# Attention rows of two batches, laid singly along the steps of the second expert

## The chip, the cores and the metric

The kernel runs on one core of a Trainium2 chip. The time is the device time of one execution in microseconds (us); the profile is of one execution of its own. A core has TensorE (PE; its weight loads are shown apart as PEld), VectorE (DVE), ScalarE (ACT), GpSimd (POOL) and SyncE (SP), whose queue issues most DMAs here. Each engine runs its own instructions in order; semaphores order the engines among each other.

## The reference

There are three stages. The first is attention with 4 batches, 8 heads, 576 rows and a head size of 64, in which a score under its row's maximum less `tau` is dropped. The attention's output, 2304 tokens of 512 values, goes through two experts of 2048 hidden values one after the other; the second one's output is the result.

```python
scores = scale * np.matmul(q, k.transpose(0, 1, 3, 2))
thresh = np.max(scores, axis=-1, keepdims=True) - tau
scores = np.where(scores >= thresh, scores, -1e9)      # then a softmax, and attn @ v
...
h = x @ w_in                                           # first expert
g = (a0 + a1*h + a2*h**2 + a3*h**3) / (1 + |b0|*|h| + |b1|*h**2 + 1e-6)
x = g @ w_out
...
h = x @ w_in                                           # second expert
g = np.where(h >= 1, h, np.where(h <= -1, 0, (h + 1)**2 / 4))
return g @ w_out
```

## The kernel before

The experts set the beat. The work is cut into 192 steps: for each of the four batches a phase of the first expert and then one of the second (`m` 0 and 1), in each phase three blocks of 192 tokens (`j`) and eight chunks of 256 hidden values (`i`), so 24 steps a phase. In the code batches count from 0, in the text from 1: batch 3 is `b` 2. Steps 48 to 71 are the first expert of batch 2, 72 to 95 its second expert, 96 to 119 and 120 to 143 the two of batch 3.

A step has a first product (L889, 24 matmuls of 192 columns), the activation, a split of the result into two half-precision parts (L210 on ScalarE, L214 on GpSimd), and three steps later (`LAG`) the second product (L905, 24 matmuls). The activation is `rational` in the first expert, with six VectorE operations (L750, L751, L752, L755, L760, L761) and ScalarE's, first of them L748; in the second expert it is `quadratic`, with one on ScalarE (L812) and two on VectorE (L813, L814). The weights lie in eight buffers; while a phase's last eight steps run, the chunks of the next expert are loaded into them, 1 MB each, from the SP queue.

Attention of the first batch stands before the steps. That of batches 2 to 4 is laid beside the steps of the batches before: the generator `attention(b)` gives work in units, and `spread` hands these out evenly over the steps in `ATTENTION`, as first step, step of the first row, and end. A batch has preparation (`prep_pair` loads two heads' q and k, scales and splits them and transposes them by DMA; `prep_v` does the same for v without a transpose) and then, for each of four pairs of heads, nine rows of scores (`ROWS`), three a unit. A row is a chain over all engines:

- scores (L397, L398, TensorE, into a PSUM tile of which there is one),
- the maximum (L445, VectorE), the two constants (L446 ScalarE, L447 VectorE),
- the exponential (L404, ScalarE) and the threshold (L405, VectorE),
- the split (L413 ScalarE, L414 and twice L416 GpSimd) into `hl`,
- a transposing DMA from the SP queue into `eT` (L418; three buffers),
- the weighted sums with v (L431, sets of 14 matmuls; the ninth row has two sets),
- after each second row and the ninth, `normalize` (L466 to L480), which transposes the result on TensorE (L471) and writes it to `xT`, the input of the first expert.

The order on each engine is made at build time by a scheduler that simulates the program and, among what is ready, issues what has the earliest priority. `at(t)` sets a priority by step. A first product has its step's, a second product 1.5 steps more, a unit of attention 1.5 steps less than its place, and the weighted sums of batches 3 and 4 three steps more than their unit. Priority is no barrier: what is ready early may be issued early. `tc.issue_after(x)` is one: what is traced under it on the engine of `x` is issued behind `x`. Before the change only the second products stand under it.

Of the kernel before, what the change touches and what calls it, by code (L numbers as in the profile page):

```python
# [10 lines left out]
F32 = mybir.dt.float32  # L11
I32 = mybir.dt.int32
BF16 = mybir.dt.bfloat16
AF = mybir.ActivationFunctionType
ALU = mybir.AluOpType
# [6 lines left out]
LARGEST = 3e38  # L22
# [12 lines left out]
N_TEMP, N_POLY, N_WT, N_WH, N_GG, N_ROW, N_SC = 5, 3, 3, 2, 4, 3, 2  # L35


PREPARE = 1, 6
ATTENTION = {1: (18, 18 + 32 * 3 / 17, 50), 2: (51, 67, 100), 3: (99, 115, 147)}
PREPARED = 3  # L40
WEIGHTS = (0, 20)


@with_exitstack
def tile_attention_moe_moe2(
# [18 lines left out]
    V, A, G, T, Q = nc.vector, nc.scalar, nc.gpsimd, nc.tensor, nc.sync  # L64
    B, H, S, D = q.shape
    P = 128
    NP = H // 2
    NT = S // P
    ST = S - NT * P
# [16 lines left out]
    ap = ctx.enter_context(tc.tile_pool(name="ap", bufs=2))  # L86
# [4 lines left out]
    ps_1 = ctx.enter_context(tc.tile_pool(name="ps_1", bufs=1, space=PSUM))  # L91
    ps_2 = ctx.enter_context(tc.tile_pool(name="ps_2", bufs=1, space=PSUM))
# [17 lines left out]
    def small(n, name, keep=False):  # L110
        if keep:
            return cp.tile([P, n], F32, name=name)
        tag = "".join(x for x in name if x.isalpha() or x == "_").rstrip("_")
        return sp.tile([P, n], F32, name=name, tag=f"s{n}_{tag}", bufs=4 if tag in ("mx", "nt") else 2)
# [38 lines left out]
    ln_e = small(1, "ln_e", True)  # L153
# [23 lines left out]
    def at(when):  # L177

        return tc.high_priority(tc.cur_priority - int(1000 * (when + 100)))
# [200 lines left out]
    ROWS = [(t, ab) for t in range(NT) for ab in range(2)] + [(NT, 0)]  # L380
    M = NT * P

    def scores(s, t, ab, qT, kT, kT2):

        if t < NT:
            parts = [(slice(0, P), ab * (NT + 1) + t, slice(0, P), [(ab * S, S)])]
        else:
            parts = [(slice(i * ST, (i + 1) * ST), NT, slice(i * ST, (i + 1) * ST),
                      [(0, S)] if i == 0 else [(S + ST, M), (S, ST)]) for i in range(2)]
        k1 = kT.rearrange("p c s -> p (c s)")  # L390
        k2 = kT2.rearrange("p c s -> p (c s)")
        for rows, c, cols, keys in parts:
            at = 0
            for k0, n in keys:
                while n:
                    w = min(n, 512 - at % 512)
                    T.matmul(s[rows, at : at + w], qT[:, c, cols], k1[:, k0 : k0 + w], start=True, stop=False)  # L397
                    T.matmul(s[rows, at : at + w], qT[:, c, cols], k2[:, k0 : k0 + w], start=False, stop=True)  # L398
                    at, k0, n = at + w, k0 + w, n - w

    def softmax(b, s, ab, con, nb, th, name):

        e = ap.tile([P, S], F32, name="e" + name, tag="e", bufs=N_SC)
        A.activation(e, s, AF.Exp, bias=nb, scale=con[:, 0:1])  # L404
        V.scalar_tensor_tensor(e, s, th, e, op0=ALU.is_ge, op1=ALU.mult)  # L405
        hl = ap.tile([P, 2 * S], F16, name="hl" + name, tag="hl", bufs=N_ROW)
        if ab == 0:

            hi, whole, half, lo_w, lo_h = hl[:, 0:S], slice(0, M), slice(M, S), hl[:, S + ST :], hl[:, S : S + ST]
        else:  # L410

            hi, whole, half, lo_w, lo_h = hl[:, S:], slice(ST, S), slice(0, ST), hl[:, 0:M], hl[:, M:S]
        A.copy(hi, e)  # L413
        G.tensor_tensor(lo_h, e[:, half], hi[:, half], op=ALU.subtract)  # L414
        for p in (slice(0, M // 2), slice(M // 2, M)):
            G.tensor_tensor(lo_w[:, p], e[:, whole][:, p], hi[:, whole][:, p], op=ALU.subtract)  # L416
        eT = ap.tile([P, C, P], F16, name="eT" + name, tag="eT", bufs=N_ROW)
        Q.dma_start_transpose(out=eT, in_=hl)  # L418
        return eT

    def weighted(pv, rows, eT, cols, vv, h, ab):

        his, los = [(c, c) for c in range(NT)], [(NT + 1 + c, c) for c in range(NT)]
        if ab:
            his, los = los, his
        blocks = []
        for c, x in [(NT, NT)] + his:
            blocks += [(c, x, 0, D + 1), (c, x, D + 1, D)]
        blocks += [(c, x, 0, D + 1) for c, x in los]
        for n, (c, x, at, w) in enumerate(blocks):  # L430
            T.matmul(pv[rows, 0:w], eT[:, c, cols], vv[:, h * NT + x if x < NT else H * NT + h, at : at + w], start=(n == 0), stop=(n == len(blocks) - 1))  # L431

    now = [0]

    def att_rows(b, pr, g, data, pvs):

        con, qT, kT, kT2, vv, h = data
        name = f"{b}_{pr}_{g}"
        rows = ROWS[3 * g : 3 * g + 3]
        for r, (t, ab) in enumerate(rows):  # L440
            banks = ps_2.tile([P, 1024], F32, name=f"s{name}_{r}", tag="s")
            scores(banks, t, ab, qT, kT, kT2)
            mx, nt = small(1, f"mx{name}_{r}"), small(2, f"nt{name}_{r}")
            s = ap.tile([P, S], F32, name=f"sc{name}_{r}", tag="sc", bufs=N_SC)
            V.tensor_scalar(s, banks[:, 0:S], 1.0, -LARGEST, op0=ALU.mult, op1=ALU.max, accum_out=mx)  # L445
            A.activation(nt[:, 1:2], mx, AF.Identity, bias=ln_e, scale=con[:, 1:2])  # L446
            V.tensor_scalar(nt[:, 0:1], mx, con[:, 2:3], None, op0=ALU.add)  # L447
            eT = softmax(b, s, ab, con, nt[:, 1:2], nt[:, 0:1], f"{name}_{r}")
            if ab == 0:
                pv = ps_1.tile([P, 512], F32, name=f"pv{b}_{pr}_{t}", tag="pv")  # L450
                pvs[t] = pv[:, 0 : 2 * (2 * D + 2)].rearrange("p (a d) -> p a d", a=2)
            with at(now[0] + 3) if b > 1 else nullcontext():
                if t < NT:
                    weighted(pvs[t][:, ab], slice(0, P), eT, slice(0, P), vv, h + ab, ab)
                else:
                    for i in range(2):
                        c = slice(i * ST, (i + 1) * ST)
                        weighted(pvs[t][:, 0], c, eT, c, vv, h + i, 0)
                if ab == 1 or t == NT:
                    normalize(b, pr, t, pvs.pop(t))  # L460

    def normalize(b, pr, t, pv):
        name = f"{b}_{pr}_{t}"
# [16 lines left out]
            V.tensor_tensor(dst[:, 1], pt[r, c : c + w], dst[:, 0], op=ALU.subtract)  # L480

    NG = len(ROWS) // 3
    N_UNITS = NP * (NG + 1) + 1

    def attention(b):

        ahead = [prep_pair(b, 0)]
        yield
        vv = prep_v(b)
        yield  # L490
        xT[b] = [xp.tile([P, 2 * KT, TB], F16, name=f"xT{b}_{j}", tag="xT", bufs=NB) for j in range(NB)]
        ahead.append(prep_pair(b, 1))
        yield
        for pr in range(NP):
            pvs = {}
            data = ahead.pop(0) + (vv, 2 * pr)
            for g in range(NG):
                att_rows(b, pr, g, data, pvs)
                yield
                if g == 1 and pr + 2 < NP:  # L500
                    ahead.append(prep_pair(b, pr + 2))
                    yield


    def first_v():
# [422 lines left out]
    def spread(first, last, units):  # L928
        for n, u in enumerate(units):
            t = first + n * (last - first) / len(units)  # L930
            beside[int(t)].append((t, u))

    for b, (first, rows, last) in ATTENTION.items():
        spread(first, rows, [("att", b)] * PREPARED)
        spread(rows, last, [("att", b)] * (N_UNITS - PREPARED))
    spread(*WEIGHTS, [("w", i, x) for i in range(NCH) for x in range(2)])

    pending, consts, accs, atts = [], {}, {}, {}
# [15 lines left out]
    for st, (n, m, b, j, i) in enumerate(steps):  # L954
        with at(st):
            if i == 0:
                if m == 0:
                    consts[m, b, j] = moe1_consts(b) if j == 0 else consts[m, b, 0]
                else:
                    if b == 0 and j == 0:  # L960
                        moe2_weights()
                    consts[m, b, j] = moe2_consts(b, j)
            gg, last = first_product(m, b, j, i, consts[m, b, j])
        pending.append((n, m, b, j, i, gg, last))
        if len(pending) > LAG:
            with at(st + 1.5):
                finish_step()
        for t, u in beside[st]:
            if u[0] == "w":
                with at(t - 3):  # L970
                    stage_half(1, u[1], u[2], False)
            else:
                if u[1] not in atts:
                    atts[u[1]] = attention(u[1])
                now[0] = t - 1.5
                with at(now[0]):
                    next(atts[u[1]])
    while pending:
        with at(st + 1.5):
# [29 lines left out]
```

## Time and profile before

| | |
|---|---|
| median of 3 executions | 1236.87 us (1236.17 to 1237.26) |
| the profiled execution | 1231.83 us, span 1230.0 us |
| PE, PEld busy | 1094.3 us (89%), 989.2 us (80%) |
| DVE busy | 977.6 us (79%) |
| ACT, POOL busy | 839.2 us (68%), 553.4 us (45%) |
| granted TensorE clock, mean | 0.965 |

The shares are means over the whole span. Which engine is full changes from phase to phase, so the rows below are cut at the phases.

### The profile page before, as it was taken

The numbers are of one execution on the slowest core, as the hardware profiler recorded it, in microseconds if no ns is written. First come the engines' busy times: TensorE is split into PE (matmuls) and PEld (weight loads), VectorE is DVE, ScalarE is ACT, GpSimd is POOL, SyncE is SP. The second block draws the span as 40 slices with busy tenths as digits, with TensorE's granted clock in tenths as the row PEclk, the third lists the DMA queues.
The fourth block names the chain that finished last, engine by engine and source line by source line (L and its number), as shares of the span: only waits on it lengthen the run. The fifth ranks groups of instructions, "written<-read, shape, count | busy, mean of one in ns | idle before, by whom it ended". The sixth has DMA issues, their size and how long they took to land.

```text
span 1230.0 us, 31762 instructions
## 1 busy us (share of the span) xinstructions
PE 1094.3 (89%) x12636; PEld 989.2 (80%) x12636; DVE 977.6 (79%) x2365; ACT 839.2 (68%) x1532; POOL 553.4 (45%) x698
## 2 busy tenths in 40 slices
PE   2878788588899999998899998988999998999998
PEld 1445555477889988997889898987888998999998
DVE  8887996999997387799995767899987777896432
ACT  2677777798886377788764776888666676775332
POOL 2445455666665166224553564234564652222221
PEclk9889888799999999999999999999999999999999
DMA  7677667644278159734492559333775476007000
GB/s 228 220 224 243 228 243 254 208 116 115 50 191 210 34 117 198 206 101 93 112 277 42 111 93 240 115 78 70 233 177 92 79 193 187 10 2 269 8 14 27
DMA packets 217845, 175.51 MB, mean 143 GB/s; under 512 B 179680, under 2 KB 190944, under 8 KB 209504
## 3 DMA queue, kind: packets, MB, share of 16 engines
q1 hardware_dynamic: 216320, 171.12, 52.5%
q8 instruction: 99, 1.62, 0.5%
q10 hardware_dynamic: 1376, 2.36, 0.5%
q14 instruction: 50, 0.41, 0.1%
HBM read 106.83 MB, written 21.50 MB: 104 GB/s over the span
## 4 chain that ended last, share of the span: by engine, by line
PE 39%; DVE 31%; ACT 10%; DMA 7%; issue 7%; POOL 5%; SPq 1%; ACTq 0%; DVEq 0%; POOLq 0%
PE acc L905 15%; PE ph L889 15%; DMA eT<-hl 3%; DVE e L405 3%; DVE t L755 3%; DVE t L750 2%; DVE sc L445 2%; PE pv L431 2%; DVE t L761 2%; POOL wh L214 2%; PE pv L617 2%; DVE t L760 2%; DVE t L751 2%; DVE t L752 2%; DVE wt L232 1%
## 5 line engine op out<-in xcount | busy, mean ns | idle before, releaser
L905 PE MATMUL acc<-gg,wc 128*128 128x192 f16 x4608 | 426.1, 247 | 12.8 <-POOL gg L214 6.1
L889 PEld LDWEIGHTS <-wc 128*128 128x128 f16 x4608 | 391.2, 99 | 30.0 <-issue 24.3
L905 PEld LDWEIGHTS <-wc 128*128 128x128 f16 x4608 | 385.0, 98 | 13.7 <-issue 12.0
L214 POOL TENSOR_TENSOR gg<-t,gg 128x384 f16<-128x384 f32 x192 | 195.9, 1023 | 382.2 <-ACT gg L210 307.9
L889 PE MATMUL ph<-xT,wc 128*128 128x192 f16 x2304 | 217.8, 252 | 14.4 <-DVE t L752 14.0
L889 PE MATMUL ph<-yT,wc 128*128 128x192 f16 x2304 | 214.4, 247 | 7.1 <-DVE t L814 4.1
L416 POOL TENSOR_TENSOR hl<-e,hl 128x256 f16<-128x256 f32 x216 | 162.5, 772 | 0.0
L210 ACT CAST gg<-t 128x384 f16<-128x384 f32 x192 | 97.1, 508 | 85.2 <-DVE t L814 44.8
L813 DVE SCALAR_TENSOR_TENSOR t<-t,c 128x384 f32<-128x384 f32 x96 | 64.6, 673 | 93.9 <-ACT t L812 92.2
L405 DVE SCALAR_TENSOR_TENSOR e<-sc,nt,e 128x576 f32<-128x576 f32 x108 | 95.1, 881 | 23.3 <-ACT e L404 22.6
L414 POOL TENSOR_TENSOR hl<-e,hl 128x64 f16<-128x64 f32 x108 | 47.4, 439 | 130.3 <-ACT hl L413 121.5
L404 ACT ACTIVATE e<-sc,nt,con 128x576 f32<-128x576 f32 x108 | 93.4, 865 | 4.8 <-POOL hl L416 0.2
L445 DVE TENSOR_SCALAR_CACHE_REDUCE sc<-s 128x576 f32<-128x576 f32 x108 | 80.8, 748 | 16.8 <-PE s L398 16.3
L812 ACT ACTIVATE t<-ph,c 128x384 f32<-128x384 f32 x96 | 64.0, 667 | 41.3 <-PE ph L889 40.9
L413 ACT CAST hl<-e 128x576 f16<-128x576 f32 x108 | 72.1, 668 | 27.4 <-DVE e L405 27.0
L431 PE MATMUL pv<-v,eT 128*128 128x65 f16 (+3 forms) x1680 | 75.1, 194 | 17.4 <-DMA eT<-hl 15.9
L431 PEld LDWEIGHTS <-eT 128*128 128x128 f16 (+1 forms) x1680 | 65.5, 100 | 24.1 <-DMA eT<-hl 18.7
L214 POOL TENSOR_TENSOR wc<-wt,wc 128x256 f16<-128x256 f32 x64 | 54.9, 890 | 61.0 <-ACT wc L210 61.0
L748 ACT ACTIVATE t<-ph,sc 128x384 f32<-128x384 f32 x96 | 55.2, 575 | 38.8 <-PE ph L889 38.2
L753 ACT ACTIVATE t<-t,lc 128x384 f32<-128x384 f32 x96 | 67.7, 708 | 19.6 <-DVE t L750 18.8
L214 POOL TENSOR_TENSOR wh<-wt,wh 128x256 f16<-128x256 f32 x64 | 59.0, 952 | 35.3 <-ACT wh L210 35.2
L750 DVE SCALAR_TENSOR_TENSOR t<-t,qc 128x384 f32<-128x384 f32 x96 | 69.1, 720 | 6.9 <-ACT t L748 6.8
(244 smaller groups left out, 1907.6 us busy)
## 6 DMA issues: line engine op xcount, KB each, us to landing
wc<-scratch SPq DMA_DIRECT2D x56, 1024.0 KB, 6.2
rw<-in_moe_w_in_dram SPq DMA_DIRECT2D x15, 1024.0 KB, 5.6
rw<-in_moe_w_out_dram SPq DMA_DIRECT2D x15, 1024.0 KB, 5.4
scratch<-wc SPq DMA_DIRECT2D x8, 1024.0 KB, 4.5
scratch<-wh SPq DMA_DIRECT2D x16, 512.0 KB, 3.6
rqk<-in_q_dram SPq DMA_DIRECT2D x16, 256.0 KB, 2.9
rqk<-in_k_dram SPq DMA_DIRECT2D x16, 256.0 KB, 3.1
kT<-qkT SPq DMA_DIRECT2D x26, 144.0 KB, 2.6
```

What stands on the lines that cost most here:

```text
L210: A.copy(hi, src)
L214: G.tensor_tensor(lo[:, p], src[:, p], hi[:, p], op=ALU.subtract)
L404: A.activation(e, s, AF.Exp, bias=nb, scale=con[:, 0:1])
L405: V.scalar_tensor_tensor(e, s, th, e, op0=ALU.is_ge, op1=ALU.mult)
L413: A.copy(hi, e)
L416: G.tensor_tensor(lo_w[:, p], e[:, whole][:, p], hi[:, whole][:, p], op=ALU.subtract)
L431: T.matmul(pv[rows, 0:w], eT[:, c, cols], vv[:, h * NT + x if x < NT else H * NT + h, at : at + w], start=(n == 0), stop=(n == len(blocks) ...
L445: V.tensor_scalar(s, banks[:, 0:S], 1.0, -LARGEST, op0=ALU.mult, op1=ALU.max, accum_out=mx)
L750: V.scalar_tensor_tensor(u, u, qc[:, 0:1], u, op0=ALU.add, op1=ALU.mult)
L753: A.activation(r, u, AF.Ln, bias=lc[:, 1:2], scale=lc[:, 0:1])
L889: last = T.matmul(ph[:, f, :], w[:, wx, kt, f * P : (f + 1) * P], rhs, start=(n == 0), stop=(n == 3 * KT - 1))
L905: T.matmul(dst, w[:, wx, f, d * P : (d + 1) * P], gg[:, gx, f, :], start=(i == 0 and f == 0 and n == 0 and d % 2 == 0), stop=(i == NCH - 1 ...
```

## The change

For batches 3 and 4 a unit is now one row in place of three, and the units of rows lie on steps 72.3 to 97 and 120.3 to 145 (before: 67 to 100 and 115 to 147). The preparation lies on the steps ahead of that. A row's weighted sums are held back and traced behind the scores of the row three later (`BEHIND`); their own priority of three steps more is gone. The last three rows' sums are a unit of their own. All units from the first row on stand under `tc.issue_after(last)`, where `last` is the last matmul of the step's first product. Batch 2 keeps three rows a unit with the sums at once.

```diff
-ATTENTION = {1: (18, 18 + 32 * 3 / 17, 50), 2: (51, 67, 100), 3: (99, 115, 147)}
+ATTENTION = {1: (18, 18 + 32 * 3 / 17, 50), 2: (51, 72.3, 97), 3: (99, 120.3, 145)}
+BEHIND = 3
...
+    def sums_of(b, pr, t, ab, h, vv, eT, pvs):
+        if ab == 0:
+            pv = ps_1.tile([P, 512], F32, name=f"pv{b}_{pr}_{t}", tag="pv")
+            pvs[t] = pv[:, 0 : 2 * (2 * D + 2)].rearrange("p (a d) -> p a d", a=2)
+        if t < NT:
+            weighted(pvs[t][:, ab], slice(0, P), eT, slice(0, P), vv, h + ab, ab)
+        else:
+            for i in range(2):
+                c = slice(i * ST, (i + 1) * ST)
+                weighted(pvs[t][:, 0], c, eT, c, vv, h + i, 0)
+        if ab == 1 or t == NT:
+            normalize(b, pr, t, pvs.pop(t))
+
+    def att_row(b, pr, r, data, pvs):
...
+        eT = softmax(b, s, ab, con, nt[:, 1:2], nt[:, 0:1], name)
+        return partial(sums_of, b, pr, t, ab, h, vv, eT, pvs)
...
-            with at(now[0] + 3) if b > 1 else nullcontext():
...
-    N_UNITS = NP * (NG + 1) + 1
+    N_UNITS = {b: NP * ((NG if b == 1 else len(ROWS)) + 1) + (1 if b == 1 else 2) for b in range(1, B)}
...
+        held = []
         for pr in range(NP):
             pvs = {}
             data = ahead.pop(0) + (vv, 2 * pr)
-            for g in range(NG):
-                att_rows(b, pr, g, data, pvs)
-                yield
-                if g == 1 and pr + 2 < NP:
+            for r in range(len(ROWS)):
+                held.append(att_row(b, pr, r, data, pvs))
+                if b == 1 or len(held) > BEHIND:
+                    held.pop(0)()
+                if b > 1 or r % 3 == 2:
+                    yield
+                if r == 5 and pr + 2 < NP:
                     ahead.append(prep_pair(b, pr + 2))
                     yield
+        for f in held:
+            f()
+        yield
...
-                now[0] = t - 1.5
-                with at(now[0]):
+                with at(t - 1.5), tc.issue_after(last) if u[1] > 1 and t >= ATTENTION[u[1]][1] else nullcontext():
                     next(atts[u[1]])
```

A batch has 42 units, 3 of preparation ahead of the rows and 39 from the first row on: 36 rows, the preparation of pairs 3 and 4, and the last sums. 39 units on 24.7 steps are 0.633 steps each.

## Rows read from the trace of the kernel before

**Rows 1.** Busy us of each engine by stretch: start:end, length, engines, granted clock, DMA share, GB/s.
```profile
495.70:551.00 55.30, 52.71 (x650) 51.07 (x648) 48.74 (x116) 45.62 (x86) 12.92 (x17) 1.00 0.57 149
551.00:624.60 73.60, 64.50 (x785) 59.95 (x784) 73.60 (x181) 57.05 (x111) 37.60 (x46) 0.98 0.51 127
624.60:762.60 138.00, 128.35 (x1690) 119.62 (x1688) 95.89 (x264) 86.10 (x166) 66.21 (x96) 0.99 0.66 144
684.70:762.60 77.90, 72.83 (x997) 66.82 (x994) 52.71 (x139) 52.87 (x101) 41.22 (x65) 1.00 0.74 162
762.60:812.30 49.70, 49.52 (x620) 48.68 (x618) 44.92 (x107) 41.71 (x80) 12.88 (x16) 1.00 0.39 114
812.30:884.30 72.00, 61.56 (x733) 57.37 (x732) 71.65 (x176) 55.74 (x108) 33.48 (x40) 0.98 0.48 114
884.30:1017.50 133.20, 129.76 (x1744) 120.90 (x1742) 101.13 (x276) 89.97 (x169) 74.21 (x104) 1.00 0.65 145
945.00:1017.50 72.50, 71.08 (x984) 65.94 (x983) 51.81 (x136) 50.95 (x95) 43.66 (x65) 1.00 0.67 146
```

**Rows 2.** The same view of L404 alone, ACT's exponential: one for each row.
```profile
495.70:624.60 128.90, 11.22 (x13) 0.99 0.53 137
...
684.70:762.60 77.90, 15.61 (x18) 1.00 0.74 162
762.60:812.30 49.70, 0.00 (x0) 1.00 0.39 114
...
762.60:884.30 121.70, 7.77 (x9) 0.99 0.44 114
...
945.00:1017.50 72.50, 15.09 (x18) 1.00 0.67 146
```

**Rows 3.** The same view of L431 alone, the weighted sums on PE and PEld.
```profile
624.60:762.60 138.00, 18.03 (x392) 15.42 (x392) 0.99 0.66 144
...
884.30:1017.50 133.20, 19.23 (x420) 16.63 (x420) 1.00 0.65 145
```

**Rows 4.** DVE by line, 551.0 to 624.6: count, busy us, mean ns, idle before.
```profile
L755 DVE SCALAR_TENSOR_TENSOR t<-t,ka,t 128x384 f32<-128x384 f32 x13 | 9.9, 761 | 0.0
L405 DVE SCALAR_TENSOR_TENSOR e<-sc,nt,e 128x576 f32<-128x576 f32 x11 | 9.5, 865 | 0.0
```

**Rows 5.** The chain of waits, 709 to 722: start us, length us, engine and line.
```profile
713.64 0.21 PE s L397
...
714.12 1.98 PE acc L905 x24
...
720.40 0.88 PE pv L431 x28
```

**Rows 6.** The chain of waits, 738 to 763, where rows follow each other.
```profile
740.00 0.78 DVE sc L445 x2
...
740.80 0.40 ACT nt L446
...
747.56 0.88 ACT e L404
...
748.46 0.88 DVE e L405
...
749.36 0.68 ACT hl L413
...
750.42 1.26 POOL hl L416 x2
```

**Rows 7.** The tile eT, 684.7 to 762.6: its DMAs from issue to landing.
```profile
DMA to landing us min/median/max: 3.2/3.5/8.9
```

**Rows 8.** Waits of the SP queue, 624 to 763: total us, times, longest.
```profile
SPq L418 <- PE pv L431: 26.0, 6, 8.0
```

**Rows 9.** The chain of waits at two places where a pair is prepared.
```profile
638.70 5.81 DMA rqk<-in_q_dram
...
827.01 5.63 DMA qkT<-qk
```

More of the change, by code (lines that the diff above doesn't have):

```diff
@@ L431, in weighted @@
             T.matmul(pv[rows, 0:w], eT[:, c, cols], vv[:, h * NT + x if x < NT else H * NT + h, at : at + w], start=(n == 0), stop=(n == len(blocks) - 1))
-    now = [0]
-    def att_rows(b, pr, g, data, pvs):
-        con, qT, kT, kT2, vv, h = data
[L438 to L451, printed above, removed]
-            with at(now[0] + 3) if b > 1 else nullcontext():
[L453 to L460, printed above, removed]
@@ new lines, in att_row @@
+    def att_row(b, pr, r, data, pvs):
+        con, qT, kT, kT2, vv, h = data
+        name = f"{b}_{pr}_{r // 3}_{r % 3}"
+        t, ab = ROWS[r]
+        banks = ps_2.tile([P, 1024], F32, name="s" + name, tag="s")
+        scores(banks, t, ab, qT, kT, kT2)
+        mx, nt = small(1, "mx" + name), small(2, "nt" + name)
+        s = ap.tile([P, S], F32, name="sc" + name, tag="sc", bufs=N_SC)
+        V.tensor_scalar(s, banks[:, 0:S], 1.0, -LARGEST, op0=ALU.mult, op1=ALU.max, accum_out=mx)
+        A.activation(nt[:, 1:2], mx, AF.Identity, bias=ln_e, scale=con[:, 1:2])
+        V.tensor_scalar(nt[:, 0:1], mx, con[:, 2:3], None, op0=ALU.add)
+        eT = softmax(b, s, ab, con, nt[:, 1:2], nt[:, 0:1], name)
+        return partial(sums_of, b, pr, t, ab, h, vv, eT, pvs)
@@ L934, in tile_attention_moe_moe2 @@
         spread(first, rows, [("att", b)] * PREPARED)
-        spread(rows, last, [("att", b)] * (N_UNITS - PREPARED))
+        spread(rows, last, [("att", b)] * (N_UNITS[b] - PREPARED))
     spread(*WEIGHTS, [("w", i, x) for i in range(NCH) for x in range(2)])
```

## The prediction

> **What bounds the kernel now.** I read three views in this order: the busy time of each engine by stretch, the instructions by line inside a stretch, and the chain of waits.
>
> The first view is cut where the program's phases begin: each phase has 24 steps, and a step shows as one L748 (first expert) or one L812 (second expert). In the second expert of batch 2 (624.6 to 762.6) and of batch 3 (884.3 to 1017.5) TensorE is the full engine: 128.35 of 138.0 us and 129.76 of 133.2 us, while VectorE has 95.89 and 101.13 [rows 1]. In the second half of the first expert it is the other way round. From 551.0 to 624.6 VectorE is busy 73.60 of 73.6 us and from 812.3 to 884.3 it is busy 71.65 of 72.0 us; TensorE has 64.50 and 61.56 there [rows 1]. These two stretches are 12 steps each, at 6.1 and 6.0 us a step. The twelve steps just before the second of them (762.6 to 812.3), with no exponential of a row in them, take 49.7 us, 4.1 a step [rows 1, 2].
>
> So which engine is the bound changes from phase to phase, and the rows of attention sit on both sides. Batch 3's rows should start at step 67, but the exponentials of 12 of its 36 rows (the stretch shows 13, the first being the last row of the batch before) ran before step 72, in the phase that VectorE bounds; of batch 4's rows 9 ran before step 120 [rows 2]. By the lines, VectorE had no idle time there before any of its big operations (idle 0.0 before L755 and L405) [rows 4]. There a row costs VectorE time on the path; in the second expert it costs TensorE time.
>
> **The change part by part.** No instruction is added or taken away: the same 36 rows a batch, each with its score matmuls, its row of softmax, one transposing DMA and its sums. What changes is the place.
>
> *Rows out of the first expert.* Each row of batches 3 and 4 is now traced behind the last matmul of its step's first product, and the first such step is 72 (or 120). No score matmul of these batches can be issued sooner, so the 12 and 9 rows leave the VectorE-bound stretches for certain. What remains there is the preparation of a batch (two pairs and v). Bounds for twelve steps with preparation and no rows: 49.7 us (762.6 to 812.3, which holds v's preparation and a pair) and 55.3 us (495.7 to 551.0, which holds the same and the tail of the batch before) [rows 1]. I take the middle, 52.5: less work is left than in the slower row, but the loads of a pair can stall as they do now [rows 9]. That gives back 73.6 − 52.5 = 21.1 us and 72.0 − 52.5 = 19.5 us, 40.6 together (36 to 46 by the bounds).
>
> *Rows into the second expert.* The phase of batch 2 goes from 36 − 12 = 24 exponentials to 36, that of batch 3 from 36 − 9 = 27 to 36 [rows 2]. The sums are sets of 14 matmuls, 40 a batch; now 392 and 420 matmuls, 28 and 30 sets, fall into these phases [rows 3]. After the change all but the last three rows' 4 sets do, so 36: 8 and 6 more. On the chain a row's four score matmuls lie between 713.64 and 714.12, where the second product goes on: 0.48 us a row. Two sets of sums, 28 matmuls, are 0.88 us, so a set is 0.44 [rows 5]. TensorE therefore gets 12 × 0.48 + 8 × 0.44 = 9.3 us and 9 × 0.48 + 6 × 0.44 = 7.0 us more, 16.3 together. As it is the bound there, I count all of that. VectorE pays 0.78 + 0.88 us a row beside small operations [rows 6]; with 12 more rows its 95.89 us become some 116 to 120 of about 147, so it does not take over.
>
> *Sums three rows behind.* Now the sums stand by priority three steps behind the scores. After it, they stand three rows behind: 39 units on 24.7 steps are 0.633 steps each, three are 1.9 steps, and with a step of about 6.0 us (144 / 24) that is 11.4 us. A row's own way, read from one row: 0.78 VectorE, 0.40 and 0.88 ScalarE, 0.88 VectorE, 0.68 ScalarE, 0.38 until GpSimd's wide operations begin at 750.42 and 1.26 for these, 5.3 us in all, and then the transposing DMA [rows 6]. It lands in 3.5 us at the median and 8.9 us at the most [rows 7]: 8.8 us in the common case, 14.2 us in the worst, which comes where the weight chunks of the next phase load. So the eT is there in time, with 2.6 us to spare, for most rows, and is up to 2.8 us late for the rows of the last eight steps. A late eT holds the sums at the head of TensorE's queue, and behind them the next first product, its ScalarE and VectorE work and the second product three steps on. Since three rows are under way, a delay of 2.8 us costs 0.9 a row: at most 12 × 0.9 = 11 us a phase, at the least nothing. As the median is nearest, I take 2 us a phase, 4 together.
>
> *Queues.* Six transposes of batch 3 waited 26.0 us on the SP queue until sums freed a buffer, with weight loads behind them [rows 8]. After the change the sums of row r−3 stand just behind the scores of row r, some 5 us before row r's transpose asks for the buffer: that wait should go. It costs TensorE little now, so I count nothing. The loads of pairs 3 and 4 move to 76.1 and 82.4 steps (now 71.7 and 81.1). Such loads have held ScalarE and then TensorE before: 5.81 us at 638.7 [rows 9]. They stay where they are in kind, at the same price as now.
>
> **The sum.** −40.6 + 16.3 + 4 = −20.3 us. The profiled execution has 1231.83 us (span 1230.0), so about 1211.5; its distance to the median (1236.87) is 5.0, and the median becomes 1217.
>
> A share by which to check the room: TensorE's weight loads fill 119.62 of 138.0 us and 120.90 of 133.2 us, its matmuls 128.35 and 129.76 [rows 1]. The Trainium skill (Perfetto Trace Analysis, Identifying the Most-Contended Engine) calls matmul busy time a poor measure of the room that is left and prefers the weight loads' share; by it the phases have 18 and 12 us of room, which would take the added 16.3 us for next to nothing, and the sum would be −36. A 512-column score matmul takes 0.22 us with a weight load of far less beside it, so part of that room is not there; I stay with the chain.
>
> **The rivals.**
>
> *The rows fill idle TensorE time* (chance 0.10). By the matmul rows the two phases have 138.0 − 128.35 = 9.7 and 133.2 − 129.76 = 3.4 us without a matmul [rows 1]. If evenly spread rows used all of it, the added work would cost 16.3 − 13.1 = 3.2 us, without further waits: −37, 1200 us. For it: idle time in the phase of batch 2 is three times that of batch 3, so it is no law. Against it: DMA waits cause part of it [rows 9].
>
> *The second expert gets slow throughout* (0.15). Rows are densest now in the second halves, 18 rows on 12 steps, 1.5 a step: 77.9 us (684.7 to 762.6) and 72.5 us (945.0 to 1017.5) [rows 1, 2]. The new density, 36 rows on 23.4 steps, is 1.54. At 72.5 a half the phases cost 290 us for 271.2, near my sum; at 77.9 a half they cost 311.6, 40.4 more, and the whole gain is gone: 1237. For it speaks that the worse half is batch 3's, against it that its 18 rows came in bursts.
>
> *Preparation binds the first expert* (0.15). At 827.0 VectorE's last preparation step is followed by 5.63 us of a transposing DMA, and the chain is in loads until ScalarE goes on at about 839 [rows 9]. If each stretch kept 7 us of this, the gain there is 26.6 and the time 1231.
>
> *Slower: the sums wait for their transposes everywhere* (0.13). Place: TensorE's queue, at the sums. If the way from a row's maximum to its eT took 13 us on average rather than 8.8, because VectorE, ScalarE and GpSimd are fuller, each row would wait (13 − 11.4) / 3 = 0.53 us, 72 rows 38 us: −40.6 + 16.3 + 38 = +14, 1251. At 14.2 us it is 1280. It decides from an average of 12.4 us on, where 72 × 0.33 eats up the 24 us. For it: the landing of 8.9; against it: the median of 3.5, and the 3.6 us between 8.8 and 12.4.
>
> **How the numbers follow.** The likeliest, 1217, has 0.47; its own range, with 36 to 46 us given back and 0 to 22 us of waits, is 1207 to 1240 at the ends, most of it below 1225. The range 1200 to 1240 leaves out the slower rival and little at the lower end. A measurement of this kernel can tell 0.2%, 2.5 us. Faster: 0.47 + 0.10 + three quarters of 0.15 for the preparation, and a third of 0.15 for the dense halves: 0.73. Same: 0.09. Slower: 0.13 and a third of the dense halves, 0.18.
>
> **What would show it.** Right: no L404 of batches 3 and 4 before their second expert begins; the two stretches of the first expert near 52 us with TensorE the full engine; second experts of 144 to 149 us; few waits of L431 for eT, and those in the last third. Wrong: L431 waiting for eT all through the phase, or first-expert stretches still near 60 us with VectorE idle behind a load.

## The result, and the profile after

The changed kernel takes 1223.12 us at the median (1218.84 to 1226.65, 4 executions), the kernel before 1236.52 (1235.26 to 1237.26): 0.9897 of it, with a 95% interval of 0.9864 to 0.9931. The forecast was 1217 us in a range of 1200 to 1240, which also holds the time before. The profiled execution has 1223.93 us (span 1222.1).

One profile is one execution, and executions of this kernel lie some us apart. The profiled one of before (1231.83) lies 4.7 us under its median, that of the changed kernel 0.8 above. So the phases below account for 1230.0 − 1222.1 = 7.9 us; the other 5.5 us of the 13.4 between the medians stand in no trace here. One execution of the weight-load version below (1273.28 us) fell in a slower state of the chip and is left out of that version's median and ratio.

Busy us of each engine by stretch in the changed kernel, cut where the same phases and half phases begin (the columns as in [rows 1]):

```profile
495.70:549.60 53.90, 50.99 (x641) 50.33 (x640) 47.62 (x111) 44.57 (x84) 11.93 (x14) 1.00 0.56 153
549.60:604.00 54.40, 50.09 (x582) 49.28 (x580) 52.70 (x134) 39.62 (x74) 13.07 (x13) 0.97 0.29 89
604.00:755.20 151.20, 140.50 (x1872) 127.40 (x1870) 118.01 (x314) 106.33 (x202) 84.78 (x130) 0.99 0.72 152
755.20:812.10 56.90, 53.12 (x647) 52.13 (x644) 50.04 (x112) 43.10 (x80) 10.84 (x14) 0.97 0.47 126
812.10:866.20 54.10, 49.12 (x584) 48.05 (x583) 52.81 (x133) 39.73 (x76) 14.10 (x14) 1.00 0.29 91
866.20:1011.40 145.20, 137.81 (x1869) 125.80 (x1868) 117.98 (x314) 105.84 (x199) 86.11 (x130) 1.00 0.72 153
```

The two VectorE-bound stretches of 73.6 and 72.0 us are now 54.4 and 54.1. VectorE is still the fuller engine in them, with 52.70 and 52.81 us beside TensorE's 50.09 and 49.12. The second experts, 138.0 and 133.2 us before, are 151.2 and 145.2.

L405, the exponential, by phase, as in [rows 2]:

```profile
495.70:604.00 108.30, 0.86 (x1) 0.98 0.42 121
604.00:755.20 151.20, 31.19 (x36) 0.99 0.72 152
755.20:866.20 111.00, 0.00 (x0) 0.98 0.38 109
866.20:1011.40 145.20, 31.20 (x36) 1.00 0.72 153
```

All 36 rows of both batches lie in the second expert (the one at 495.7 belongs to the batch before). The sums, as in [rows 3]:

```profile
604.00:755.20 151.20, 21.88 (x504) 19.31 (x504) 0.99 0.72 152
866.20:1011.40 145.20, 21.32 (x504) 18.90 (x504) 1.00 0.72 153
```

504 matmuls are 36 sets, the number that was forecast. The score matmuls (the tile `s`) on TensorE in the two second experts, first the kernel before, then the changed one:

```profile
624.60:762.60 138.00, 15.47 (x104) 0.99 0.66 144
884.30:1017.50 133.20, 18.16 (x120) 1.00 0.65 145
...
604.00:755.20 151.20, 24.19 (x160) 0.99 0.72 152
866.20:1011.40 145.20, 23.40 (x160) 1.00 0.72 153
```

The waits of the weighted sums on TensorE for their eT in the same four phases (total us, times, longest):

```profile
PE pv L431 <- DMA eT<-hl: 3.0, 2, 2.2
...
PE pv L431 <- DMA eT<-hl: 1.4, 1, 1.4
...
PE pv L432 <- DMA eT<-hl: 5.1, 6, 1.2
...
PE pv L432 <- DMA eT<-hl: 3.0, 5, 1.1
```

So the sums wait for their eT 8.1 us in place of 4.4. The SP queue's wait for a buffer in the second expert of batch 2, 26.0 us in [rows 8], is 7.0:

```profile
SPq L419 <- PE pv L432: 7.0, 3, 2.6
```

### The profile page after: what moved, and what is told of

Same layout as the page of the kernel before. It is cut to its first block, busy times and chain, and to the rows that moved or that the text cites. A ratio compares the mean times of both kernels' runs of the same rounds, so it can differ in the third digit from the quotient of the medians.

```text
span 1222.1 us, 31762 instructions
## 1 busy us (share of the span) xinstructions
PE 1086.5 (89%) x12636; PEld 983.2 (80%) x12636; DVE 983.5 (80%) x2365; ACT 842.6 (69%) x1532; POOL 536.2 (44%) x698
## 4 chain that ended last, share of the span: by engine, by line
PE 39%; DVE 26%; DMA 11%; ACT 10%; issue 7%; POOL 6%; SPq 1%; ACTq 0%; DVEq 0%; POOLq 0%
PE acc L912 15%; PE ph L896 14%; DMA eT<-hl 7%; POOL wh L215 2%; DVE e L406 2%; DVE t L762 2%; PE pv L432 2%; PE pv L624 2%; DVE t L757 2%; DVE t L768 2%; DVE sc L456 2%; POOL hl L417 2%; DVE t L758 1%; DMA rqk<-in_k_dram 1%; DVE qk L218 1%
## 5 line engine op out<-in xcount | busy, mean ns | idle before, releaser
L912 PE MATMUL acc<-gg,wc 128*128 128x192 f16 x4608 | 424.3, 247 | 13.2 <-DVE mye L191 7.5
L215 POOL TENSOR_TENSOR gg<-t,gg 128x384 f16<-128x384 f32 x192 | 193.0, 1007 | 400.7 <-ACT gg L211 342.1
L417 POOL TENSOR_TENSOR hl<-e,hl 128x256 f16<-128x256 f32 x216 | 152.5, 727 | 0.0
L406 DVE SCALAR_TENSOR_TENSOR e<-sc,nt,e 128x576 f32<-128x576 f32 x108 | 103.2, 956 | 29.6 <-ACT e L405 28.7
L414 ACT CAST hl<-e 128x576 f16<-128x576 f32 x108 | 72.3, 669 | 41.1 <-DVE e L406 32.0
L405 ACT ACTIVATE e<-sc,nt,con 128x576 f32<-128x576 f32 x108 | 93.5, 866 | 6.0 <-ACT nt L457 0.4
L415 POOL TENSOR_TENSOR hl<-e,hl 128x64 f16<-128x64 f32 x108 | 43.0, 399 | 121.0 <-ACT hl L414 115.1
L432 PE MATMUL pv<-v,eT 128*128 128x65 f16 (+3 forms) x1680 | 71.7, 194 | 20.8 <-DMA eT<-hl 16.1
L760 ACT ACTIVATE t<-t,lc 128x384 f32<-128x384 f32 x96 | 67.8, 708 | 21.0 <-DVE t L757 20.3
L762 DVE SCALAR_TENSOR_TENSOR t<-t,ka,t 128x384 f32<-128x384 f32 x96 | 68.6, 714 | 10.2 <-ACT t L761 9.6
```

Of the source, the lines that this page charges most:

```text
L215: G.tensor_tensor(lo[:, p], src[:, p], hi[:, p], op=ALU.subtract)
L760: A.activation(r, u, AF.Ln, bias=lc[:, 1:2], scale=lc[:, 0:1])
L762: V.scalar_tensor_tensor(s, s, ka[:, 0:1], r, op0=ALU.add, op1=ALU.mult)
L912: T.matmul(dst, w[:, wx, f, d * P : (d + 1) * P], gg[:, gx, f, :], start=(i == 0 and f == 0 and n == 0 and d % 2 == 0), stop=(i == NCH - 1 ...
```

## The experiments

Each kernel was timed against the kernel before on the same chip. The first theory, "place", is that of the prediction: the rows gain by leaving the stretches that VectorE bounds. Its rival, "order", says that the new form of the rows gains (one by one, sums three behind), wherever they stand.

**The form without the tie.**

```diff
-                with at(t - 1.5), tc.issue_after(last) if u[1] > 1 and t >= ATTENTION[u[1]][1] else nullcontext():
+                with at(t - 1.5):
```

> The changed kernel without issue_after for the rows: steps, single rows and sums three behind stay. Place theory (the gain is that rows leave the VectorE-bound half of the first expert): the scheduler hoists scores again, exponentials of batches 3 and 4 appear before their second expert (5 or more a batch), and the time lies at 1228 to 1237 us. Order theory (the gain is that single rows are laid evenly and sums stand three rows behind, wherever they are): 1223, as the changed kernel, with the rows where they like.

1224.84 us, 0.9923 (0.9886 to 0.9961). The scheduler did bring rows forward, 6 − 1 and 8 exponentials into the first experts:

```profile
497.30:617.10 119.80, 5.17 (x6) 0.97 0.46 118
...
758.60:876.10 117.50, 6.93 (x8) 0.99 0.51 131
```

The first of the six belongs to the batch before. The time hardly rose. That speaks against place alone.

**The place and the tie without the form.**

```diff
-ATTENTION = {..., 2: (51, 67, 100), 3: (99, 115, 147)}
+ATTENTION = {..., 2: (51, 72.3, 97), 3: (99, 120.3, 145)}
-                with at(now[0]):
+                with at(now[0]), tc.issue_after(last) if u[1] > 1 and t >= ATTENTION[u[1]][1] else nullcontext():
```

(against the kernel before)

> The kernel before with the new steps and with issue_after for its units, but still three rows a unit and the sums three steps behind. Place theory: no exponential before the second expert, and 1219 to 1227 us, most of the gain. Order theory: 1233 to 1240, near the kernel before.

1234.19 us, 0.9987 (0.9965 to 1.0010): no gain that can be told. Yet the rows moved just as in the changed kernel, and the phases moved with them:

```profile
498.70:607.10 108.40, 99.67 (x1221) 98.24 (x1219) 99.98 (x245) 84.27 (x158) 24.96 (x27) 1.00 0.42 121
607.10:759.50 152.40, 141.27 (x1890) 127.71 (x1889) 118.73 (x314) 106.00 (x202) 82.08 (x129) 1.00 0.68 152
759.50:865.80 106.30, 99.83 (x1208) 97.28 (x1206) 100.61 (x243) 83.02 (x157) 26.76 (x29) 1.00 0.38 111
865.80:1014.40 148.60, 139.59 (x1871) 126.46 (x1870) 118.67 (x313) 104.67 (x198) 82.63 (x130) 1.00 0.70 151
```

TensorE waits for eT more often than in the changed kernel, in the two second experts:

```profile
PE pv L431 <- DMA eT<-hl: 10.1, 13, 1.4
...
PE pv L431 <- DMA eT<-hl: 8.8, 11, 1.5
```

That is 18.9 us in 24 waits, against 8.1 in 11. These traces do not show, however, that the waits are what the version loses. The four phases above sum to 515.7 us, and so do the changed kernel's (108.3, 151.2, 111.0 and 145.2). The 3.1 us between the two spans (1225.2 and 1222.1) lie almost wholly ahead of them: the first phase starts at 498.7 in place of 495.7. This execution, 1226.95 us, was the quickest of ten; what makes the median 7 us higher stands in no trace.

**Rows from step 67 and 115, tied.**

```diff
-ATTENTION = {..., 2: (51, 72.3, 97), 3: (99, 120.3, 145)}
+ATTENTION = {..., 2: (51, 67, 97), 3: (99, 115, 145)}
```

> The changed kernel with the rows' first step back at 67 and 115 (end kept): single, tied, sums three behind. 39 units on 30 steps are 0.77 a unit, so some 6 rows a batch fall into the first expert. Place theory: the change gained 13.4 us on 21 rows, 0.64 a row, so 12 rows back cost some 8 us: 1231 (1227 to 1235). Order theory: 1223 or a little less, since the rows are spread more evenly.

1222.40 us, 0.9897 (0.9866 to 0.9928), as the changed kernel, with 6 rows of each batch in the first expert. Phases:

```profile
497.00:614.70 117.70, 105.95 (x1274) 102.15 (x1271) 107.53 (x259) 91.75 (x173) 34.82 (x41) 0.99 0.45 117
614.70:752.70 138.00, 133.75 (x1809) 124.45 (x1808) 106.82 (x300) 98.24 (x188) 80.19 (x119) 0.99 0.71 159
752.70:870.40 117.70, 109.15 (x1288) 105.25 (x1286) 108.40 (x258) 91.68 (x171) 35.83 (x41) 0.96 0.41 111
870.40:1009.90 139.50, 133.79 (x1810) 124.04 (x1808) 107.35 (x299) 97.54 (x184) 77.52 (x119) 0.99 0.71 153
```

Beside the changed kernel's phases (108.3, 151.2, 111.0, 145.2) the first experts are 9.4 and 6.7 us longer and the second 13.2 and 5.7 shorter: 12 rows cost 16.1 us on one side and free 18.9 on the other. By these sums a row's price is 1.3 us where VectorE is full and 1.6 us at the end of a crowded second expert, so it is no lower there. The figures are rough: each version has one profile, and the second experts alone give 2.2 us a row for the one and 0.95 for the other. Of the 18.9 us, 10.8 are TensorE's matmul time (140.50 and 137.81 against 133.75 and 133.79) and 8.1 are time in which it stood idle.

**Batch 2 in the same way.**

```diff
-ATTENTION = {1: (18, 18 + 32 * 3 / 17, 50), ...
+ATTENTION = {1: (18, 24.3, 49), ...
...
-                if b == 1 or len(held) > BEHIND:
+                if len(held) > BEHIND:
-                if b > 1 or r % 3 == 2:
-                    yield
+                yield
```

(and the same units and tie for all three batches)

> The changed kernel with batch 2 treated in the same way (rows from step 24.3 to 49 in place of 18 + 5.6 to 50, single, tied, sums three behind). 16 exponentials of batch 2 ran in the first expert of batch 1, where VectorE is full as well. Place theory: 16 rows at 0.64 us give 10 us, 1213 (1206 to 1218), with the first expert of batch 1 shorter by 15 to 25 us and its second expert longer by 10 to 15. Rival: the conversion of the second expert's weights, which runs beside the first expert of batch 1, fills VectorE and GpSimd anyway, and the time stays within 3 us of 1223.

1226.71 us, 0.9925 (0.9898 to 0.9951): no further gain. The first and the second expert of batch 1:

```profile
224.30:345.80 121.50, 100.75 (x1102) 95.60 (x1100) 114.58 (x248) 98.68 (x182) 68.36 (x67) 0.94 0.34 107
345.80:493.10 147.30, 137.96 (x1863) 125.43 (x1861) 116.91 (x312) 106.66 (x203) 86.52 (x132) 1.00 0.74 155
```

The changed kernel has 138.1 and 127.8 us there: 16.6 given back, 19.5 paid. The first expert became shorter, as the place theory had it. The weights' conversion did not hold it, so the rival named in the expectation fell as well; the second expert took the gain.

After these four, "form" had to be taken apart: rows one by one, and sums three behind.

**Rows one by one, sums by priority.**

```diff
-                if b == 1 or len(held) > BEHIND:
+                with at(now[0] + 3) if b > 1 else nullcontext():
                     held.pop(0)()
...
+                now[0] = t - 1.5
```

> The changed kernel with each row's sums traced at once and given, as before the change, the priority of three steps more; steps, single rows and issue_after stay. The kernel before with the new places alone stayed at 1234 us, so the form of the rows is what gains; this run parts its two halves. Even theory (rows one by one in place of bursts of three): 1223, as the changed kernel. Behind theory (sums tied three rows behind their scores): 1230 to 1236.

1228.97 us, 0.9958 (0.9935 to 0.9981). The sums waited 11.4 and 10.7 us for eT, and the time lies between the two theories' numbers:

```profile
PE pv L432 <- DMA eT<-hl: 11.4, 10, 1.9
...
PE pv L432 <- DMA eT<-hl: 10.7, 12, 1.6
```

**Three rows a unit, sums three behind.**

```diff
-    N_UNITS = {b: NP * ((NG if b == 1 else len(ROWS)) + 1) + (1 if b == 1 else 2) for b in range(1, B)}
+    N_UNITS = {b: NP * (NG + 1) + (1 if b == 1 else 2) for b in range(1, B)}
-                if b > 1 or r % 3 == 2:
+                if r % 3 == 2:
```

> The changed kernel with three rows a unit again (15 units from the first row on), places, issue_after and sums three rows behind kept. Even theory: 1230 to 1236, as with the new places alone. Behind theory: 1223.

1225.97 us, 0.9922 (0.9892 to 0.9953), with waits for eT of 16.1 us:

```profile
PE pv L432 <- DMA eT<-hl: 6.5, 7, 2.4
...
PE pv L432 <- DMA eT<-hl: 9.6, 8, 3.1
```

This is neither theory's number alone, but most of the gain is here: the sums three behind bring 0.0065 with bursts (0.9987 to 0.9922) and 0.0061 with single rows (0.9958 to 0.9897). Single rows bring 0.0029 and 0.0025, which the intervals do not clear.

**Sums one row behind.**

```diff
-BEHIND = 3
+BEHIND = 1
```

> The changed kernel with the sums one row behind. A row's way to its eT is some 8.8 us, one unit is 3.8 us, three are 11.4. Behind theory: sums come to the head of TensorE's queue before their eT, 1228 us or more and more waiting of the sums for eT than in the changed kernel (5.1 and 3.0 us in the two second experts). Even theory: the scheduler puts the sums where they are ready, 1221 to 1225.

1228.88 us, 0.9947 (0.9924 to 0.9969), and 10.7 and 9.2 us of waits for eT: the waits are back, as the behind theory had it, and about half of the gain is gone at the medians (the intervals still meet).

**The preparation of pairs 3 and 4 held back on ScalarE.**

```diff
                 if r == 5 and pr + 2 < NP:
-                    ahead.append(prep_pair(b, pr + 2))
+                    with tc.issue_after(act[0]) if b > 1 else nullcontext():
+                        ahead.append(prep_pair(b, pr + 2))
...
-        A.activation(u, p, AF.Relu, bias=bias, scale=su)
+        act[0] = A.activation(u, p, AF.Relu, bias=bias, scale=su).ins
```

It was made for two pieces of the changed kernel's chain of waits, behind which ScalarE's first operation on a pair goes on at 570.9:

```profile
560.19 3.92 DMA qkT<-qk
...
567.12 3.68 DMA rqk<-in_k_dram
...
570.91 0.09 ACT qk L347
```

> The changed kernel with the ScalarE work of preparing pairs 3 and 4 queued behind the activation of the step at which it is placed (76.1 and 82.4), so that it can't be issued ahead of its loads in the first expert. In the changed kernel ScalarE waits there for pair 3's load, and the chain runs over the transpose and the loads from 560.2 to 571.5 and from 819.7 to 829.3. Preparation theory: the first experts of batches 2 and 3 lose 3 to 6 us each, the second experts gain little: 1215 (1211 to 1219). Rival: VectorE is full there in any case (0.96 to 0.99 busy in these steps) and the time stays within 3 us of 1223.

1224.65 us, 0.9904 (0.9880 to 0.9928): no gain. The first experts took 107.8 and 109.9 us for 108.3 and 111.0. So the load on the chain is not what sets the time; the rival held.

**The form alone.** By now the open question was whether the form gains without the place.

```diff
-ATTENTION = {..., 2: (51, 72.3, 97), 3: (99, 120.3, 145)}
+ATTENTION = {..., 2: (51, 67, 97), 3: (99, 115, 145)}
-                with at(t - 1.5), tc.issue_after(last) if u[1] > 1 and t >= ATTENTION[u[1]][1] else nullcontext():
+                with at(t - 1.5):
```

> The changed kernel's single rows and sums three behind, with the first steps of the kernel before (67 and 115, end 97 and 145) and without issue_after, so that rows run ahead into the first expert as far as the scheduler likes. Slack theory (the gain is that sums three rows behind leave a late transposing DMA some 2 us before TensorE waits): 0.988 to 0.993 of the kernel before, with 5 or more exponentials a batch in the first expert and few sums that wait for eT. Place theory: 0.996 to 1.001, as the rows are back where VectorE is full.

1233.64 us, 0.9988 (0.9965 to 1.0012): the number of the place theory. By the exponentials (L405, the first two lines), 12 and 8 rows ran in the first expert (the thirteenth is the batch before's), which takes 132.6 and 122.0 us again, and the sums wait little, 2.6 and 1.5 us. This execution, 1228.42 us, was the quickest of twelve:

```profile
496.40:629.00 132.60, 11.25 (x13) 1.00 0.57 135
757.60:879.60 122.00, 6.93 (x8) 0.97 0.46 123
...
496.40:629.00 132.60, 116.67 (x1450) 109.92 (x1449) 125.92 (x307) 105.53 (x200) 49.02 (x60) 1.00 0.57 135
...
757.60:879.60 122.00, 113.22 (x1357) 108.05 (x1354) 116.16 (x281) 97.67 (x182) 42.29 (x47) 0.97 0.46 123
```

**Sums four rows behind.**

```diff
-BEHIND = 3
+BEHIND = 4
```

> The changed kernel with the sums four rows behind; there are still three eT buffers, so a row's transpose waits for sums that now stand one row later. Slack theory: the sums find their eT landed nearly always (TensorE's waits for eT below the 5.1 and 3.0 us of the changed kernel), the transposes wait more for buffers on the SP queue (above 7.0 and 8.7 us), and the time is 0.986 to 0.991 of the kernel before. Rival (buffers): the buffer wait holds the SP queue and the weight loads in it, 0.993 or more.

1221.83 us, 0.9892 (0.9862 to 0.9922), no difference that can be told from three. The waits for eT are 3.6 and 4.6 us, the second longer than the slack theory had it; the transposes' wait for a buffer grew from 7.0 and 8.7 us to:

```profile
SPq L419 <- PE pv L432: 22.9, 11, 5.3
...
SPq L419 <- PE pv L432: 24.1, 12, 5.5
```

**The weight loads from ScalarE's queue.**

```diff
-        Q.dma_start(wc, scratch[m][i])
+        A.dma_start(wc, scratch[m][i])
```

> The changed kernel with the weight chunks' loads issued from ScalarE's queue in place of SyncE's. It tells what makes a transpose late in the first and last third of a second expert. If it is the order in one queue (a transpose behind a 1 MB load), the eT lands in 3.2 to 3.9 us at the median and 5 at the most, and the time falls to 1215. If it is the sixteen DMA engines that both share, the landing stays at 7 us and more at its longest and the time does not fall; it rises to 1226 or more where a load waits for its buffer at the head of ScalarE's queue.

1252.77 us, 1.0160 (1.0121 to 1.0198). The transposes did not land sooner; in the second expert of batch 2 the longest took 12.0 us in place of 7.6, and the sums waited 11.9 us for eT in place of 5.1:

```profile
DMA to landing us min/median/max: 3.2/3.4/12.0
```

So taking the loads out of the queue does not make a transpose land sooner. The expectation's other reading, that loads and transposes share the DMA engines, is left, but no run shows it by itself.

**Early start and four behind together.**

```diff
-ATTENTION = {..., 2: (51, 72.3, 97), 3: (99, 120.3, 145)}
-BEHIND = 3
+ATTENTION = {..., 2: (51, 67, 97), 3: (99, 115, 145)}
+BEHIND = 4
```

> The changed kernel with the first rows at steps 67 and 115, tied, and the sums four rows behind: the two variants that were as fast as the changed kernel, together. If what is left of waits for eT in each (9.6 us with the early start, 8.2 with four rows behind, 8.1 in the changed kernel) can still be cut by having more room, 0.984 to 0.988 of the kernel before. Rival: the waits for eT that are left come from the weight loads and stay, and the transposes wait for their three buffers instead: 0.989 as both are alone.

1229.99 us, 0.9969 (0.9941 to 0.9997): slower than either alone, a miss for both expectations. In the profiled execution (1234.47 us) the second expert of batch 3 has a wait that no other run has:

```profile
PE xt L471 <- DVE c L807: 6.3, 1, 6.3
```

TensorE stood 6.3 us for VectorE there, and the transposes waited 26.9 us for buffers. Whether that is what costs this version its gain was not tried; this execution lies 4.5 us above the median, so the wait may be its own. No version beat the changed kernel by more than can be told.

## Why the prediction was right, and where it was not

*Rows out of the first expert*: right. No exponential of batches 3 and 4 ran there, and the two stretches came to 54.4 and 54.1 us, between the bounds of 49.7 and 55.3. Contrary to the prediction, TensorE did not become the full engine there: VectorE is busy 97 and 98% of the two. The term was too large all the same. The sum took the stretch just before (762.6 to 812.3, 49.7 us) as given, and that one grew to 56.9 us; the one at 495.7 fell by 1.4. Over the whole first experts 20.6 (128.9 to 108.3) and 10.7 us (121.7 to 111.0) came back, 31.3 in place of 40.6. Of the 7.2 us more between 755.2 and 812.1, 3.6 are matmul time (53.12 for 49.52 us, with 27 more matmuls inside the cut), and 3.6 are time in which TensorE stood idle; the longest wait there is one of 2.9 us for VectorE. Why VectorE was late is open: the preparation of pairs 3 and 4 was tried as a cause and gave nothing.

*Rows into the second expert*: the counts of exponentials and sets were right (36 and 36), the price too low. 13.2 and 12.0 us came on, 25.2 in place of 20.3 with the waits, and the first of the two phases, 151.2 us, is over the 144 to 149 that were named. TensorE's matmul time rose by 12.15 and 8.05 us, 20.2 in place of 16.3. The sums took 5.9 us of that, about as counted (6.2). The score matmuls took 14.0 in place of 10.1: they are 96 more, 24 times four where 21 were counted, since the ninth row of a pair has eight, and four of them took 0.58 us in place of 0.48. The transposes of `normalize` on TensorE (L471), six more and 1.45 us, were not counted. The other 5.0 us are time without a matmul.

*Sums three rows behind*: in the new places the waits of the sums for eT are of the size that was forecast, 8.1 us for 4.4, 3.7 more where 4 were taken. Their place was not: the prediction looked for late transposes in the last third, where the next weights load, and 5.8 of the 8.1 us lie in the first third of the two phases (3.0 us up to 652, 2.8 up to 914). Weight loads run there too, as the last section shows.

*The sum*: −31.3 + 25.2 is −6.1 and the rest of the span −1.8, so −7.9 in the profiles, −13.4 at the medians; −20.3 was forecast. The rows moved as in the likeliest case, two terms were mis-sized, and the gain has a condition that the prediction did not see, the next point. The range is no proof of the mechanism, as it holds the time before as well. The prediction took 0.2% as what can be told; the interval of the result is 0.34% to either side.

*The gain was put on the place alone*, and that does not hold. Place and tie alone have 18.9 us of waits of the sums for eT and end at 0.9987; form alone has few waits and ends at 0.9988, its rows back in the first expert; both together give 0.9897. Neither half of the change gains by itself as far as can be told, and neither of my two first theories holds alone. The rival that ended slower named TensorE's queue at the sums as the place where it is decided; the prediction counted the sums three behind as a cost of 0 to 11 us a phase; against what the new places would have had without them they are most of the gain, 0.0061 to 0.0065 of the time. With single rows the waits are shorter by it (22.1 to 8.1 us); with bursts they hardly are (18.9 to 16.1). Four rows behind shorten them no further (8.2 us). That the waits are the gain is not shown, and two things speak against it: in units of three, waits of 16.1 us went with 0.9922, and the profile with 18.9 us of waits has phases that are no longer. How the sums three behind gain stays open.

*The tie or the steps*: that rows start at 72.3 rather than 67 does not matter. With the tie the early start is as fast; without it and with the late start (0.9923) most of the gain is there too. Only with the early start and no tie do rows run as far ahead as before.

*Queues*: the buffer wait on the SP queue fell from 26.0 to 7.0 us, as forecast; when four rows behind brought 22.9 back, the time stayed, so counting nothing for it was right.

*Weight loads' share as the room left*: by that share 18 and 12 us were free, and these rows did not get them. The shares were 87 and 91% before and are 127.40 / 151.20 = 84% and 125.80 / 145.20 = 87% with the 21 rows, and the phases got longer by more than the added matmul time. The Trainium skill (Perfetto Trace Analysis, Identifying the Most-Contended Engine) judges TensorE's headroom by MFU, the useful share of its peak rate, and by the weight loads' share; as a measure of room for these rows, the trace does not bear out the second.

## What to carry to other kernels

Moving work from a phase that one engine bounds to a phase that another bounds gains the difference of the two marginal prices. Here the price in the new phase was higher at its crowded end (some 1.6 us a row for the last 12, by two profiles) than on average (25.2 us for 21 rows, 1.2 each), so an instruction's own time understates it. How the work is ordered in its new place counted as much as the place: sums a fixed three rows behind did better than sums ordered by priority, with the same rows in the same phases. Try the halves of a change apart, since here neither alone gained anything that could be told. And look at the whole stretch before a wait is called the cause: here 18.9 us of waits and 8.1 us went with phases of the same length.

## What the runs showed of the hardware

Transposing DMAs landed later where 1 MB loads ran beside them. In the changed kernel's second expert of batch 2, from 604 to 652 us, with four such loads, the median landing is 4.8 us; from 652 to 700, with none, it is 3.2; from 704 to 755.2, with four again, it is 3.9:

```profile
wc<-scratch SPq DMA_DIRECT2D x4, 1024.0 KB, 5.9
...
eT<-hl SPq DMA_TRANSPOSE x9, 4.8
...
eT<-hl SPq DMA_TRANSPOSE x12, 3.2
```

Loads issued from ScalarE's queue did not change that for the better: over the whole phase the longest landing was 12.0 us, 7.6 with one queue, at medians of 3.4 and 3.5.

Executions of one program scatter: the changed kernel's lay within 1218.84 to 1226.65 us, those of the new places alone within 1226.95 to 1238.92, so a single profile of these can be 7 us off its median. Part of that goes with the granted TensorE clock, as a mean over the span: the two quickest with the new places alone (1226.95 and 1229.85 us) had 0.969 and 0.968, the two slowest (1237.55 and 1238.92) 0.963.
